# V of four batches formed from weights in SBUF, and sread's features turned once

## The chip, the cores and the metric

The kernel runs on one core of one Trainium2 chip. The metric is the device time of one execution in microseconds (us). Weights, inputs and outputs lie in the chip's DRAM; the core works on SBUF tiles of 128 partitions and collects matmul results in PSUM. Its engines are TensorE (PE, with the weight load PEld beside it), VectorE (DVE), ScalarE (ACT) and GpSimd (POOL); SyncE (SP) issues most of the DMAs of this kernel, POOL some, ACT the stores of results.

## The reference

The shapes are 8 batches, 8 heads, 512 positions, a state of 32 rows per head, D = 64, model width 512, hidden width 2048.

```python
scores = scale * np.matmul(x, state.transpose(0, 1, 3, 2))
...
xread = np.matmul(a, state)                       # a: softmax of scores
scores2 = scale * np.matmul(state, x.transpose(0, 1, 3, 2))
...
sread = np.matmul(a2, x)                          # a2: softmax of scores2
attn_out = np.concatenate([xread, sread], axis=2)
x = attn_out.transpose(0, 2, 1, 3).reshape(B * S, H * D)      # 8 x 544 tokens x 512
h = x @ w_in
g = np.where(h >= 1, h, np.where(h <= -1, 0.0, (h + 1) ** 2 / 4))
x = g @ w_out
h = x @ w2_in
g = np.maximum(h, 0.0) + alpha * np.minimum(h, 0.0)
out = g @ w2_out
```

## The kernel before, in words

The kernel has two phases. This case touches only the first: attention and the first pair of matrix products (`w_in`, `w_out`). The second phase (`hB`, `accB`) starts about half way through.

**Precision.** A float32 product is made as three matmuls on a high and a low part of each operand (high·high, high·low, low·high): `mm3`. ACT makes the high part (L73), DVE the low part (L76). Weights arrive as 64-bit floats: a raw tile `wr_…` (L302) is decoded into `wf_…` by one ACT pass (L309) and four DVE passes (L318, L320, L323, L326), then split into `w_…h` and `w_…l`.

**Stages and steps.** The first phase is 9 stages t of 16 steps f; step i = 16·t + f, and `gi(t, f)` is its number. Each step makes 128 hidden columns: `h_mm(i + 2)` fills `hA`, `act_fn` makes `g`, `g_split` its parts `gh` and `gl`, `out_mm(i)` adds to four `accA`. Stages 0 to 7 are the 512 xread rows of batches 0 to 7, stage 8 the 256 sread rows of all batches. In stage 0 the `accA` products take one matmul each (L516), from stage 1 on three (L524).

**V.** For xread the state and `w_in` are multiplied first: V[t, blk, q] = state of batch t times the 512 columns `blk` of `w_in`, four heads in each q, and `hA` is V times the attention weights `at…`. V of batch 0 is made from the parts of `w_in` in SBUF (`vdirect`). For batches 1 to 4 (group 0) and 5 to 7 (group 1) V is made in groups: `stg` holds the state of four batches, transposed and split into `sts…h` and `sts…l`. The parts of `w_in` are first stored to DRAM as `wd` (L372). For each `blk` and head, POOL loads the 64 rows of that head, high parts over low parts, into one tile `ws` (L408), PE makes two matmuls with it (L416, L417), ACT copies the result to `vgo` (L419), and SP stores that to DRAM as `vd` (L420). `vr_load` (L426) fetches the rows of one batch back when its stage is near.

**sread.** Its rows come out of the attention with the features in another order (tile `xsf`), so `w1s_load` (L450) reads 128 rows of `wd` in that order: four runs of 32 rows each per tile. 32 such loads, `w1s…h` and `w1s…l`, feed `hA` of stage 8. `xs_hi` and `xs_lo` make the parts `xsh` and `xsl`.

**What sets the order.** Side work is put at a step by `at(step, function, …)`; a loop over the steps emits it beside the main work, and a scheduler orders each engine's instructions from there. An SP DMA that has to wait for data or for a free buffer holds up all that stands behind it in SP's queue. `up` is a pool of 80 tiles of 128x512, `vp` one of 10 tiles of 128x1024 (raw weights, `x`, `x2h`, `x2l`, `stg`, `xsf`).

Of the kernel before, what the change touches and what calls it, by code (L numbers as in the profile page):

```python
# [9 lines left out]
F32 = mybir.dt.float32  # L10
# [21 lines left out]
NB, NH, S, NS, D = 8, 8, 512, 32, 64  # L32
# [8 lines left out]
def kernel_body(ctx: ExitStack, tc: tile.TileContext, x, state, w1i, w1o, w2i, w2o, alpha, out):  # L41
# [9 lines left out]
    def U(name, dt=F32):  # L51
        return up.tile([128, 512], dt, tag="u", name=name)

    def V(name, dt=F32):
        return vp.tile([128, 1024], dt, tag="v", name=name)
# [4 lines left out]
    def PS(name):  # L60
        return pp.tile([128, 512], F32, tag="ps", name=name)
# [37 lines left out]
    GRP = [1, 4]  # L99
# [6 lines left out]
    XS = {}  # L106
# [188 lines left out]
    W = {}  # L295
    VW = {}
    ST = {}
# [87 lines left out]
            VW[b, blk, q] = (h, l)  # L385

    def ld_stg(g):
        t = V(f"stg{g}")
        tv = t.rearrange("p (h u d) -> p h u d", h=NH, u=2)
        for i in range(4):  # L390
            for u in range(2):
                ld.dma_start(out=tv[32 * i:32 * i + 32, :, u, :],
                             in_=state[GRP[g] + i].rearrange("h n d -> n h d"))
        G["stg", g] = t

    def st_build(g, hh):
# [9 lines left out]
    def vg_load(g, blk, h):  # L406
        t = U(f"ws{g}{blk}{h}", F32R)
        pool.dma_start(out=t, in_=wd[blk][:, h * D:(h + 1) * D, :])  # L408
        G["w", g, blk, h] = t

    def vg_mm(g, blk, h):
        ws = G.pop(("w", g, blk, h))
        sh, sl = ST[g, h // 4]
        c = (h % 4) * 128
        ps = PS(f"vgp{g}{blk}{h}")
        pe.matmul(ps, sh[:, c:c + 128], ws, start=True, stop=False)  # L416
        pe.matmul(ps, sl[:, c:c + 128], ws, start=False, stop=True)  # L417
        o = U(f"vgo{g}{blk}{h}")
        act.copy(o, ps)  # L419
        ld.dma_start(out=vd[g][blk][h], in_=o)  # L420

    def vr_load(b, blk, q):
        g = 0 if b < 5 else 1
# [20 lines left out]

    def w1s_load(blk, c):
        h, l = U(f"w1s{blk}{c}h", F32R), U(f"w1s{blk}{c}l", F32R)
        o = (c // 2) * 256 + (c % 2) * 32
        for k, t in enumerate((h, l)):
            src = wd[blk][k, (c // 2) * 256:(c // 2 + 1) * 256, :]
            ld.dma_start(out=t.bitcast(F32), in_=src.rearrange("(h e i) f -> h e i f", h=4, e=2)[:, c % 2])  # L450
        W["w1s", blk, c] = (h, l)


# [2 lines left out]
    def gi(t, f):  # L456
        return t * NF + f
# [334 lines left out]
    def at(i, fn, *a):  # L792
        side[i].append((fn, *a))

    def xs_hi(c):
        if c == 0:
            XS["h"], XS["l"] = V("xsh", F32R), V("xsl", F32R)
        s = slice(c * 256, (c + 1) * 256)
        hi_(XS["h"][:, s], XS["f"][:, s])
# [22 lines left out]
    def vg_plan(g, start, per):  # L822
        n = 0
        for blk in range(4):
            for h in range(NH):
                o = start + int(n * per)
                at(o - 2, vg_load, g, blk, h)
                at(o + 1, vg_mm, g, blk, h)
                n += 1
        at(start - 2, ld_stg, g)  # L830
        at(start, st_build, g, 0)
        at(start, st_build, g, 1)

    vg_plan(0, gi(0, 2), 0.5)
    vg_plan(1, gi(2, 0), 1.0)

    for blk in (1, 2, 3):
# [9 lines left out]
    for f in range(NF):  # L847
        at(gi(1, f - 3), dec_hi, ("w1o", f))
        at(gi(1, f - 2), dec2, ("w1o", f))
    for c in range(4):  # L850
        at(gi(7, c), xs_hi, c)
        at(gi(7, c + 1), xs_lo, c)
    for blk in range(4):
        for c in range(4):
            at(gi(8, 4 * blk - 9 + c), w1s_load, blk, c)

    w2 = [("w2i", n // 2, n % 2) for n in range(16)] + [("w2o", f) for f in FO]
    for n, key in enumerate(w2):
        o = gi(1, 6) + int(3.2 * n)
        at(o - 3, d_load, key, src_w2p(*key[1:]) if key[0] == "w2i" else src_w2o(key[1]))  # L860
        decode(key, o)
        if key[0] == "w2i":
            at(o + 4, w2i_store, *key[1:])
        else:
            at(o + 1, w2o_put, key[1])
            at(o + 5, w2o_store, key[1])
# [91 lines left out]
```

## Time and profile before

| what | us |
|---|---|
| median of 3 runs | 1504.56 |
| lowest, highest | 1504.22, 1504.85 |
| the profiled execution | 1504.31 |
| its span | 1502.5 |
| PE busy in it | 1410.2 |
| DVE busy | 1045.4 |
| ACT busy | 782.5 |
| POOL busy | 111.2 |

The profiled execution is one run of its own; its time is the device time, its span the part between the first and the last instruction in the trace. The view by stretches cuts that span: stage 0 runs from about 34 to 190 us, stage 1 from 190 on, stage 8 from about 700 to 783. PEclk is the granted clock of TensorE as a share of its full speed. Matmuls are pipelined, so the distance between the starts of two of them, not the length of one, tells what each adds.

### The profile page before, as it was taken

The page shows a single profiled execution, that of the slowest core. Times are in us where ns is not written, and L with a number is a line of the kernel's source. Part 1 is how long each engine was busy: PE and PEld are TensorE (multiplying, and loading weights), DVE is VectorE, ACT ScalarE, POOL GpSimd, SP SyncE. Part 2 cuts the span into 40 slices and gives each one's busy share as a digit, 9 for nine tenths or more (in the row PEclk, how much of TensorE's full clock was granted, in tenths as well). Part 3 has the DMA queues.
Part 4 walks back from the last instruction along what each step waited for, and adds up shares of the span by engine and source line. Part 5 has one row for each costly group of instructions (what it writes and reads, how often), then busy time and mean ns, then how long its engine had stood idle before and what let it go on. Part 6 is the DMA issues. An engine that isn't in the chain of part 4 may idle for free.

```text
span 1502.5 us, 18956 instructions
## 1 busy us (share of the span) xinstructions
PE 1410.2 (94%) x6460; PEld 1166.7 (78%) x6460; DVE 1045.4 (70%) x1889; ACT 782.5 (52%) x1498; POOL 111.2 (7%) x125
## 2 busy tenths in 40 slices
PE   4689799899999999999779999999999999999997
PEld 2355488688888888888668878888888888989886
DVE  7687388677778788853448787666866787687641
ACT  3365577567677777764435354333533454354431
POOL 1112101112100000000110020000100010010000
PEclk8889899999999999999889999999999999999999
DMA  7999645687844444443231335344544554654554
GB/s 238 293 289 325 194 146 146 191 224 218 232 156 139 149 154 137 148 155 130 108 116 61 119 140 180 122 157 152 196 141 167 198 205 167 204 193 177 189 177 159
DMA packets 180089, 262.72 MB, mean 175 GB/s; under 512 B 76824, under 2 KB 88600, under 8 KB 179992
## 3 DMA queue, kind: packets, MB, share of 16 engines
q1 hardware_dynamic: 107720, 235.45, 46.7%
q0 software_dynamic: 66560, 17.01, 6.5%
q10 hardware_dynamic: 5712, 9.05, 1.6%
q8 instruction: 51, 0.84, 0.2%
q14 instruction: 46, 0.38, 0.1%
HBM read 205.66 MB, written 55.57 MB: 174 GB/s over the span
## 4 chain that ended last, share of the span: by engine, by line
PE 80%; DMA 10%; DVE 7%; ACT 2%; issue 1%; SPq 0%; POOL 0%; ACTq 0%; DVEq 0%; POOLq 0%
PE accB L733 22%; PE accA L524 21%; PE hB L668 20%; PE hA L84 11%; DMA wr_wi<-in_moe_w_in_dram 2%; DMA x<-in_x_dram 2%; DMA wr_w1o<-in_moe_w_out_dram 2%; PE accA L516 1%; PE sr L84 1%; PE sc L84 1%; DMA w1s33l<-wd 1%; DMA w1s13h<-wd 1%; DMA w1s23l<-wd 1%; DVE xl L76 1%; PE vgp L416 1%
## 5 line engine op out<-in xcount | busy, mean ns | idle before, releaser
L733 PE MATMUL accB<-wv,gs 128*128 128x512 f32 x1632 | 397.4, 391 | 0.2
L733 PEld LDWEIGHTS accB<-wv,gs 128*128 128x128 f32 x1632 | 305.1, 188 | 60.6 <-DVE gs L76 1.1
L668 PE MATMUL hB<-xh,wh 128*128 128x384 f32 (+1 forms) x640 | 217.9, 361 | 5.2 <-ACT p L697 2.9
L668 PE MATMUL hB<-xl,wh 128*128 128x384 f32 (+1 forms) x560 | 200.7, 358 | 0.0
L668 PE MATMUL hB<-xh,wl 128*128 128x384 f32 (+1 forms) x480 | 171.3, 360 | 0.0
L492 DVE SCALAR_TENSOR_TENSOR g<-y,hA 128x512 f32<-128x512 f32 (+1 forms) x144 | 93.6, 650 | 88.2 <-ACT y L490 87.7
L668 PEld LDWEIGHTS hB<-xh,wh 128*128 128x128 f32 x640 | 119.9, 188 | 22.5 <-DVE u L693 4.5
L76 DVE TENSOR_TENSOR gl<-g,gh 128x512 fp32r<-128x512 f32 (+1 forms) x128 | 89.1, 696 | 54.0 <-ACT gh L73 52.4
L489 ACT ACTIVATE y<-hA 128x512 f32<-128x512 f32 (+1 forms) x144 | 82.6, 574 | 73.2 <-PE hA L84 73.2
L668 PEld LDWEIGHTS hB<-xl,wh 128*128 128x128 f32 x560 | 105.5, 188 | 12.5
L677 ACT ACTIVATE m<-u 128x384 f32<-128x384 f32 (+1 forms) x80 | 45.4, 568 | 130.7 <-DVE u L693 130.7
L76 DVE TENSOR_TENSOR gs<-u,gs 128x384 fp32r<-128x384 f32 (+1 forms) x80 | 49.6, 621 | 69.5 <-ACT gs L73 69.2
L668 PEld LDWEIGHTS hB<-xh,wl 128*128 128x128 f32 x480 | 90.4, 188 | 7.8
L73 ACT CAST gh<-g 128x512 fp32r<-128x512 f32 (+1 forms) x128 | 75.7, 592 | 36.7 <-DVE g L492 31.7
L490 ACT ACTIVATE y<-y 128x512 f32<-128x512 f32 (+1 forms) x144 | 87.5, 608 | 4.2
L73 ACT CAST gs<-u 128x384 fp32r<-128x384 f32 (+1 forms) x80 | 44.4, 557 | 86.6 <-PE accB L733 85.5
L693 DVE TENSOR_TENSOR u<-hB,p 128x384 f32<-128x384 f32 (+1 forms) x80 | 48.6, 607 | 42.2 <-PE hB L668 37.4
L516 PE MATMUL accA<-g,wf_w1o 128*128 128x512 f32 x128 | 62.9, 627 | 8.1 <-DVE g L492 8.1
L679 DVE SCALAR_TENSOR_TENSOR u<-m,beta_sb,u 128x384 f32<-128x384 f32 (+1 forms) x80 | 53.4, 668 | 23.0 <-ACT m L677 22.3
L408 POOL DMA_DIRECT2D ws<-wd x64 | 50.4, 793 | 222.6 <-DMA wd<-w_wi_0l 31.0
L76 POOL TENSOR_TENSOR xl<-xr,xh 128x384 fp32r<-128x384 f32 (+1 forms) x15 | 18.7, 1247 | 630.9 <-ACT xh L73 365.2
L419 ACT COPY vgo<-vgp 128x512 f32<-128x512 f32 x64 | 36.7, 588 | 46.8 <-PE vgp L417 45.3
(916 smaller groups left out, 3045.0 us busy)
## 6 DMA issues: line engine op xcount, KB each, us to landing
wv<-wod SPq DMA_DIRECT2D x160, 512.0 KB
wr<-wid SPq DMA_DIRECT2D x80, 256.0 KB
x<-in_x_dram SPq DMA_DIRECT2D x32, 512.0 KB
ws<-wd POOLq DMA_DIRECT2D x64, 256.0 KB, 13.5
vd<-vgo SPq DMA_DIRECT2D x64, 256.0 KB
vr<-vd SPq DMA_DIRECT2D x56, 256.0 KB
out_dram<-oB SPq DMA_DIRECT2D x34, 256.0 KB
wr_wi<-in_moe_w_in_dram SPq DMA_DIRECT2D x16, 512.0 KB
```

The lines of the kernel that those rows point to most:

```text
L73: act.copy(h, raw)
L76: (eng or dve).tensor_tensor(out=l, in0=raw, in1=h.bitcast(F32), op=ALU.subtract)
L84: pe.matmul(ps, a, b, start=(k == 0), stop=(k == n - 1))
L408: pool.dma_start(out=t, in_=wd[blk][:, h * D:(h + 1) * D, :])
L489: act.activation(out=y[:, :n], in_=ps, func=AF.Relu, bias=0.5, scale=0.5)
L490: act.activation(out=y[:, :n], in_=y[:, :n], func=AF.Square)
L492: dve.scalar_tensor_tensor(out=g[:, :n], in0=y[:, :n], scalar=1.0, in1=ps, op0=ALU.min, op1=ALU.max)
L516: pe.matmul(ACC[k], w[:, k * 128:(k + 1) * 128], g, start=(f == 0), stop=(f == NF - 1))
L524: pe.matmul(ACC[k][:, :n], a, b, start=(f == 0 and j == 0), stop=(f == NF - 1 and j == 2))
L668: pe.matmul(ps, a[:, kk], b, start=(p in (0, 5, 4) and m == 0), stop=(m == 5), skip_group_check=True)
L679: dve.scalar_tensor_tensor(out=g, in0=m, scalar=beta_sb[:, f:f + 1], in1=h, op0=ALU.mult, op1=ALU.add)
L733: pe.matmul(OA[k], a, b, start=(r == 0 and j == 0), stop=(r == NF - 1 and j == 2))
```

## The change

Three things change.

First, V of group 0. `stg` is filled with zeros by POOL, and of each batch only heads of one parity are loaded into each half, so that a transposed block of `stg` has 128 rows of which 64 belong to a head and 64 are zero. With that, `vg_dir` multiplies straight with the parts of `w_in` in SBUF (128 rows, two heads), three matmuls for each head. The `ws` loads of group 0 are gone, and the matmuls for each result are three in place of two. The copy and the store stay (`vg_out`). `stg` is loaded at step −2 (was 0) and transposed at step 0 (was 2). The results come at other steps: before two heads a step from step 3 to 18, now 4, 4, 6, 6, 2, 2, 2, 2, 2, 2 heads in steps 1 to 10. Group 1 stays as it was.

Second, sread. At the last step of stage 6, `xs_turn` copies `xsf` into a new tile `xst` by 16 transfers of 32 partitions x 256 columns within SBUF, after which the features stand in their natural order; `w1s_load` reads 128 plain rows of `wd`. `xs_hi` and `xs_lo` are two steps later.

Third, the 32 decodes of the second phase's weights start at step gi(2, 4) in place of gi(1, 6), 2.75 steps apart in place of 3.2.

```diff
     def ld_stg(g):
         t = V(f"stg{g}")
         tv = t.rearrange("p (h u d) -> p h u d", h=NH, u=2)
+        if g == 0:
+            pool.memset(t, 0.0)
         for i in range(4):
             for u in range(2):
-                ld.dma_start(out=tv[32 * i:32 * i + 32, :, u, :],
-                             in_=state[GRP[g] + i].rearrange("h n d -> n h d"))
+                hs = slice(u, NH, 2) if g == 0 else slice(0, NH)
+                ld.dma_start(out=tv[32 * i:32 * i + 32, hs, u, :],
+                             in_=state[GRP[g] + i, hs].rearrange("h n d -> n h d"))
...
+    def vg_out(g, blk, h, ps):
+        o = U(f"vgo{g}{blk}{h}")
+        act.copy(o, ps)
+        ld.dma_start(out=vd[g][blk][h], in_=o)
+
+    def vg_dir(blk, c):
+        for h in (2 * c, 2 * c + 1):
+            sh, sl = ST[0, h // 4]
+            k = slice((h % 4) * 128, (h % 4) * 128 + 128)
+            ps = PS(f"vgp0{blk}{h}")
+            mm3(ps, [(sh[:, k], sl[:, k], *W["wi", blk, c])])
+            vg_out(0, blk, h, ps)
...
     def vg_mm(g, blk, h):
...
-        o = U(f"vgo{g}{blk}{h}")
-        act.copy(o, ps)
-        ld.dma_start(out=vd[g][blk][h], in_=o)
+        vg_out(g, blk, h, ps)
...
     def w1s_load(blk, c):
         h, l = U(f"w1s{blk}{c}h", F32R), U(f"w1s{blk}{c}l", F32R)
-        o = (c // 2) * 256 + (c % 2) * 32
         for k, t in enumerate((h, l)):
-            src = wd[blk][k, (c // 2) * 256:(c // 2 + 1) * 256, :]
-            ld.dma_start(out=t.bitcast(F32), in_=src.rearrange("(h e i) f -> h e i f", h=4, e=2)[:, c % 2])
+            ld.dma_start(out=t.bitcast(F32), in_=wd[blk][k, c * 128:(c + 1) * 128, :])
...
+    def xs_turn():
+        f, XS["f"] = XS["f"], V("xst")
+        for q in range(2):
+            for k in range(4):
+                for e in range(2):
+                    p, c = ((k % 2) * 2 + e) * 32, (2 * q + k // 2) * 256
+                    ld.dma_start(out=XS["f"][p:p + 32, c:c + 256],
+                                 in_=f[32 * k:32 * k + 32, (2 * q + e) * 256:(2 * q + e + 1) * 256])
...
-    vg_plan(0, gi(0, 2), 0.5)
+    at(-2, ld_stg, 0)
+    at(0, st_build, 0, 0)
+    at(0, st_build, 0, 1)
+    for blk in range(4):
+        for c in range(4):
+            at(max(1 + c, 4 * blk - 5 + c), vg_dir, blk, c)
     vg_plan(1, gi(2, 0), 1.0)
...
+    at(gi(6, 15), xs_turn)
     for c in range(4):
-        at(gi(7, c), xs_hi, c)
-        at(gi(7, c + 1), xs_lo, c)
+        at(gi(7, c + 2), xs_hi, c)
+        at(gi(7, c + 3), xs_lo, c)
...
-        o = gi(1, 6) + int(3.2 * n)
+        o = gi(2, 4) + int(2.75 * n)
```

The order of the instructions moves at three places. The rows give the line, the operation, the tile written and the tiles read; the numbers at the end of a name count the program's tiles.

First place, PE in stage 0, from the end of `hA` of step 4 on (`sc` are the attention's scores of the next batch, `stp` the transposes of `stg`, `vgp` the products of group 0). Before:

```order
L84 MATMUL hA_546<-ath_281,vw011l 128x512
L168 MATMUL sc_553<-xt_462,bdf_358 128x512
L401 MATMUL stp_562<-ident,stg_434 128x128 x4
L401 MATMUL stp_571<-ident,stg_434 128x128 x4
L516 MATMUL accA_474<-g_516,wf_w1o_403 128x512
L516 MATMUL accA_475<-g_516,wf_w1o_403 128x512
L84 MATMUL hA_611<-ath_273,vw010h 128x512
```

Now:

```order
L84 MATMUL hA_585<-ath_281,vw011l 128x512
L168 MATMUL sc_592<-xt_469,bdf_358 128x512
L168 MATMUL sc_592<-xt_477,bdf_358 128x512
L84 MATMUL vgp_597<-w_wi_1h,sts00h 128x512
L84 MATMUL vgp_597<-w_wi_1l,sts00h 128x512
L84 MATMUL vgp_597<-w_wi_1h,sts00l 128x512
L84 MATMUL vgp_604<-w_wi_1h,sts00h 128x512
L84 MATMUL vgp_604<-w_wi_1l,sts00h 128x512
L84 MATMUL vgp_604<-w_wi_1h,sts00l 128x512
L531 MATMUL accA_489<-g_473,wf_w1o_379 128x512
```

The transposes of `stg` have moved ahead of this place, and six `vgp` matmuls stand here that came later and as pairs before.

Second place, SP in stage 0, around the loads of the weights of block 2 (`wd_92` is block 1 of the stored parts). Before:

```order
L372 DMA wd_92<-w_wi_3h 128x512
L372 DMA wd_92<-w_wi_3l 128x512
L302 DMA wr_wi_2_498<-in_moe_w_in_dram 128x512
L302 DMA wr_w1o_502<-in_moe_w_out_dram 128x512
L127 DMA x_11_556<-in_x_dram 128x1024
```

Now:

```order
L372 DMA wd_92<-w_wi_3h 128x512
L420 DMA vd_0_80<-vgo_508 128x512
L420 DMA vd_0_80<-vgo_515 128x512
L420 DMA vd_1_81<-vgo_522 128x512
L420 DMA vd_1_81<-vgo_529 128x512
L372 DMA wd_92<-w_wi_3l 128x512
L302 DMA wr_wi_2_537<-in_moe_w_in_dram 128x512
L302 DMA wr_w1o_541<-in_moe_w_out_dram 128x512
L127 DMA x_11_595<-in_x_dram 128x1024
```

Four `vd` stores now stand ahead of these weight loads; before, the first `vd` store came later.

Third place, DVE in stage 1, around the pass that makes `x2l` of batch 3 (L76, 128x1024), whose end frees a buffer of `vp`. Before, in the middle of a decode of `w2i`:

```order
L318 TENSOR_SCALAR wf_w2i_1_2130<-wf_w2i_1_2130 128x512
L320 TENSOR_SCALAR wf_w2i_1_2130<-wf_w2i_1_2130 128x512
L76 TENSOR_TENSOR gl_2133<-g_2082,gh_2132 128x512
L323 SCALAR_TENSOR_TENSOR wf_w2i_1_2130<-wr_w2i_1_2040,wf_w2i_1_2130 128x512
L492 SCALAR_TENSOR_TENSOR g_2135<-y_2136,hA_2101 128x512
L76 TENSOR_TENSOR vw210l<-vr_2034,vw210h 128x512
L326 SCALAR_TENSOR_TENSOR wf_w2i_1_2130<-wr_w2i_1_2040,wf_w2i_1_2130 128x512
L76 TENSOR_TENSOR x2l_2571<-x_30_2376,x2h_2492 128x1024
```

Now:

```order
L76 TENSOR_TENSOR w_w1o_13l<-wf_w1o_1145,w_w1o_13h 128x512
L76 TENSOR_TENSOR gl_1946<-g_1891,gh_1945 128x512
L507 SCALAR_TENSOR_TENSOR g_1948<-y_1949,hA_1915 128x512
L76 TENSOR_TENSOR vw201l<-vr_1843,vw201h 128x512
L76 TENSOR_TENSOR x2l_2503<-x_30_2304,x2h_2425 128x1024
```

The pass stands behind `g` of step 32 before and behind `g` of step 29 now, and no decode of `w2i` is left ahead of it.

## Rows read from the trace of the kernel before

**Rows 1.** The page: busy time of each engine, and the granted clock in 40 equal slices of the span.

```profile
PE 1410.2 (94%) x6460; PEld 1166.7 (78%) x6460; DVE 1045.4 (70%) x1889; ACT 782.5 (52%) x1498; POOL 111.2 (7%) x125
...
PEclk8889899999999999999889999999999999999999
```

**Rows 2.** The view by stretches: start and end in us, length, busy time (and instructions) of PE, PEld, DVE, ACT and POOL, the granted clock, the DMA engines' busy share, GB/s.

```profile
34.00:78.00 44.00, 26.73 (x78) 14.69 (x76) 31.09 (x60) 17.69 (x33) 6.26 (x8) 0.87 1.19 298
78.00:108.00 30.00, 28.36 (x93) 17.33 (x94) 26.83 (x52) 19.91 (x38) 4.70 (x6) 0.90 0.92 288
108.00:160.00 52.00, 40.18 (x134) 24.59 (x133) 33.53 (x70) 25.51 (x50) 8.82 (x11) 0.93 1.09 308
160.00:190.00 30.00, 30.00 (x92) 17.59 (x91) 12.38 (x20) 18.48 (x34) 4.52 (x5) 0.96 0.63 183
190.00:290.00 100.00, 93.49 (x425) 77.23 (x425) 74.94 (x130) 70.21 (x130) 9.13 (x10) 0.97 0.50 152
507.60:572.00 64.40, 64.40 (x301) 53.76 (x300) 53.52 (x96) 45.67 (x83) 2.34 (x2) 1.00 0.44 140
700.00:783.00 83.00, 64.58 (x436) 59.81 (x435) 33.08 (x57) 31.56 (x75) 9.37 (x7) 0.88 0.30 108
```

**Rows 3.** Waits of PE in stage 8, 700 to 850 us: what waited, for what, us in total, times, the longest. The first and the last of the nine on `w1s` loads, which are 3.1, 2.3, 2.2, 2.0, 2.0, 1.8, 1.8, 1.4 and 1.1.

```profile
PE hA L84 <- DMA w1s32l<-wd: 3.1, 1, 3.1
...
PE hA L84 <- DMA w1s21l<-wd: 1.1, 1, 1.1
```

**Rows 4.** The loads of stage 8. From SP's timeline (start, length, instruction) the first issue; from the DMA view of 720 to 765 us the busy share in 40 slices (tenths) and the rates; then the mean rate of the same view of 786 to 788 us, where a load of `wr` with plain rows goes by.

```profile
667.71 0.53 SPq L450 DMA_DIRECT2D w1s00h<-wd  x1
...
DMA  2222222222222222222222232222239995222200
GB/s 102 102 102 102 102 104 100 104 102 102 102 96 104 102 102 102 102 102 102 102 102 102 102 115 104 104 102 102 95 120 279 320 224 149 98 102 102 97 35 20
...
DMA packets 265, 0.64 MB, mean 318 GB/s; under 512 B 22, under 2 KB 139, under 8 KB 265
```

**Rows 5.** PE's timeline at the start of the work on sread (start, length, instruction): two matmuls of half width in a row.

```profile
702.34 0.28 PE L84 MATMUL hA<-xsl,w1s00h 128*128 128x256 f32 x1
702.46 0.28 PE L84 MATMUL hA<-xsh,w1s00l 128*128 128x256 f32 x1
```

**Rows 6.** Stage 1: the wait of PE in 190 to 290 us, and pieces of the chain in 240 to 300 us (start, us, what).

```profile
PE accA L524 <- ACT gh L73: 6.5, 1, 6.5
...
249.87 1.37 PE hA L84 x6
...
258.97 1.24 DVE x2l L76
...
260.27 12.95 DMA x<-in_x_dram
...
275.40 4.52 PE accA L524 x12
```

**Rows 7.** Stage 0: pieces of the chain in 0 to 195 us (start, us, what).

```profile
56.83 7.40 DMA stg<-in_state_dram
...
142.88 13.21 DMA x<-in_x_dram
...
189.76 2.72 PE accA L524 x12
```

**Rows 8.** PE's timeline in stage 0: the first and the last of three groups with over 7 us of idle time before them, which stands in brackets with what ended it.

```profile
51.85 6.09 PE L516 MATMUL accA<-g,wf_w1o 128*128 128x512 f32 x8 [7.26 <-DVE g L492]
...
158.52 0.80 PE L416 MATMUL vgp<-ws,sts00h 128*128 128x512 f32 x1 [9.29 <-DVE g L492]
```

**Rows 9.** The DMA view of 0 to 160 us: all packets, POOL's queue q0 (packets, MB, time as a share of 16 engines' span), and two of the issues (count, size).

```profile
DMA packets 51351, 45.49 MB, mean 284 GB/s; under 512 B 33181, under 2 KB 36144, under 8 KB 51344
...
q0 software_dynamic: 28305, 7.18, 28.3%
...
ws<-wd POOLq DMA_DIRECT2D x28, 256.0 KB, 20.2
...
vd<-vgo SPq DMA_DIRECT2D x17, 256.0 KB
```

**Rows 10.** SP's queue in stage 0: its timeline around the loads of `stg`, and its waits for `vgo` in 0 to 190 us (us in total, times, the longest).

```profile
37.46 0.33 SPq L127 DMA_DIRECT2D x<-in_x_dram  x1
46.44 0.33 SPq L372 DMA_DIRECT2D wd<-w_wi_0h  x1
...
53.89 8.84 SPq L392 DMA_DIRECT2D stg<-in_state_dram  x8
...
SPq L420 <- ACT vgo L419: 32.2, 10, 10.1
```

**Rows 11.** The price of single instructions: one matmul of full width of group 0 from the chain at 171 us, the copy of their result (count, busy us and mean ns, idle time before it), and a zero fill on POOL.

```profile
171.72 0.23 PE vgp L416
...
L419 ACT COPY vgo<-vgp 128x512 f32<-128x512 f32 x64 | 36.7, 588 | 46.8 <-PE vgp L417 45.3
...
6.40 0.53 POOL L356 MEMSET z<- 128x512 f32 x1
```

**Rows 12.** The groups of instructions, different shapes apart: one pass of the decodes of `w2i` (count, busy us and mean ns, idle time before them).

```profile
L323 DVE SCALAR_TENSOR_TENSOR wf_w2i<-wr_w2i,wf_w2i 128x512 int32<-128x512 int32 x16 | 12.6, 790 | 0.1
```

## The prediction

> **What bounds the kernel now.** I read the page's busy line first: the matmul engine (PE) is busy 94% of the span; the granted clock is below full in two places, the first fifth and around the middle [rows 1]. Then the table by stretches: from 507 to 572 us, a piece of stage 6, PE is busy in every microsecond at full clock, and no faster transfer can shorten such a piece. There are three other places [rows 2]. Stage 0 (34 to 190 us): PE is idle for 17.3 + 1.6 + 11.8 us in the three stretches to 160 and full in the last one, at a clock of 0.87 to 0.96. Stage 1 (190 to 290): idle 6.5 us. Stage 8 (700 to 783): busy 64.6 of 83.0 us, clock 0.88. The waits of stage 8 name one cause: nine waits of PE for `w1s` tiles, from 3.1 down to 1.1 us, 17.7 us together [rows 3]. The idle time of stage 1 is one wait for `gh`, and the chain leads from there back over a single `x` load of 12.95 us, issued when a DVE pass over `x2l` freed its buffer [rows 6]. In stage 0 the chain is mostly loads, and the waits of PE in it are of 7 to 9 us each [rows 7, 8].
>
> **Stage 8: the w1s loads.** 32 loads of 256 KB. In the 45 us where hardly anything else moves, the profile has 102 GB/s at a DMA busy share of two tenths: four fifths of the engines' time lies empty [rows 4]. A load with 128 plain rows on both sides (`wr`, at 786 us) comes at 318 GB/s mean [rows 4]. So the 8.4 MB take 82 us now and would take 26 us. The first is issued at 667.7 us, the last is needed near 737 us if PE doesn't wait, so there are some 69 us: too few now, ample then. What would be late next is PE itself. Stage 8 has 384 matmuls of half width, 0.12 us apart [rows 5], and the window 52 more of full width at 0.23 us [rows 11]: 46.1 + 12.0 = 58.1 us at full clock. The whole gain is at most 83.0 − 58.1 = 24.9 us, of which 17.7 are the waits named and the rest is cold clock and small waits; a gain of the named waits alone, with the clock left as it is, would be 17.7. The clock is full in the piece of stage 6 where PE has no waits [rows 2], so I take nearly all: **−23** (−18 to −25).
>
> [...]
>
> **What is moved for it.** The features of sread are turned by 16 transfers of 32 KB at the last step of stage 6, and `xs_hi` and `xs_lo` come two steps later. 16 issues at 0.33 [rows 10] to 0.53 us [rows 4] are 5 to 9 us of SP in a stage in which no engine but PE is full; what is queued behind them are loads with several steps of lead. ACT reads the turned tile three steps later, PE 15 steps later (a step is 2.72 + 1.37 = 4.1 us [rows 6, 7]). I count them at **0**; the other end, if all 9 us held up a load that PE waits for, is +9, which I keep for the range only, since in that stage no PE wait for a load shows before.
>
> **Stage 0: V of batches 1 to 4.** Added on PE: each of the 32 products now takes three matmuls instead of two, 32 × 0.23 us = **+7.3 us** [rows 11]. Removed: 32 loads of 256 KB by POOL. What they cost is not on POOL, it is on the transfer engines. Up to 160 us, 45.49 MB go by at a mean 284 GB/s [rows 9], with a busy share of the DMA engines of 1.19, 0.92 and 1.09 in the three stretches [rows 2] (queues overlap, so it passes 1); the stretch is bound by transfers. 28 of the 32 loads lie in it, 7.3 MB. Against that, all 32 `vd` stores are now due by step 10, where 17 lay in this stretch before: +15 × 256 KB = 3.9 MB. Net 3.4 MB less, at 284 GB/s **12 us less**. The bounds: PE is idle for 30.7 us between 34 and 190 [rows 2]; the added matmuls fill 7.3 of these, and no more than the other 23.4 can be gained. On the other side, if the loads that PE waits for come no earlier, the 7.3 us of matmuls fall where PE was already full: +7.3. The order shows where they fall (first place): behind `hA` of step 4, where before stood two transposes and two `accA`, PE now has six `vgp` matmuls, and twenty heads stand in the first four steps, 60 matmuls or 13.8 us. Those are the stretches with 17.3 idle us, so most of it fills holes. The wait of 9.29 us near the end of the stage [rows 8] hangs on the `x` load of 13.21 us behind a late `wd` store [rows 7], and stays in part. I take the value that the bytes give, **−12** (−8 to −16 as its own range), net of the matmuls: it leaves 30.7 − 7.3 − 12 = 11.4 us of idle time, about that last wait and a little.
>
> The batched state `stg` now comes two steps earlier. Its eight issues held SP 8.84 us, and its landing stands in the chain with 7.40 us between two weight loads [rows 7, 10]. Before it, SP has a gap of 8.6 us between 37.8 and 46.4 [rows 10], which takes them. In the order `stg` is then ahead of the weight loads it stood between. The zero fill on POOL is twice the 0.53 us of the fill of `z` [rows 11]; POOL is idle there. On ACT the 32 copies of 588 ns [rows 11] are the same as before, only earlier. So **0** for these, with the 7.4 us of chain as an upside that is part of the bound of 23.
>
> **Stage 1.** Since the decodes of w2 start 14 steps later, DVE reaches `x2l` behind `g` of step 29 instead of 32 (order, third place). That pass releases the buffer of the late `x` load [rows 6]; three steps of 4.1 us are 12.3, the load takes 12.95, and ACT wants it at the same step as before. So the wait of 6.5 us goes all but a little, and with it the slow group behind it (12 `accA` in 4.52 us [rows 6], at full clock 2.72 [rows 7]): at most −8.3. At the least 0, if the load is held by transfers beside it. I take **−7**.
>
> **Stages 2 to 7.** The same 32 decodes are packed into 2.75 steps each instead of 3.2. DVE has 53.5 us of work in a piece of 64.4 us [rows 2]; a decode is four passes of about 0.79 us [rows 12], 3.2 us, one every 11.3 us now against 13.1 before: +2.5 us per 64 us, 87% of the time. PE stays the bound; I allow **+1** for small waits (0 to +3).
>
> **Sum.** −23 − 12 − 7 + 1 = −41 us on the profiled execution's own 1504.31 us (its span 1502.5 and 1.8 around it), which lies 0.25 us under the median of the runs: 1463.3, **about 1463 us**. With each term at its own ends: 1455 to 1474.
>
> **Rivals.**
> - Stage 0 gives nothing: SP's new order has four `vd` stores between two halves of a `wd` store and ahead of the next weight loads (order, second place), each waiting for its ACT copy (before: ten such waits, 32.2 us [rows 10]), so the loads that PE waits for come no earlier, and the added matmuls cost 0 to 7.3. For it: the stores now stand in the very steps where the weight loads are late. Against it: each load is asked for a step before its first decode and several before PE wants it, and fewer bytes go by. 1475 to 1483 us. Chance 0.17.
> - Stage 0 gives all that the PE bound allows, 22 to 23 instead of 12, since the chain's loads queue behind POOL's many small packets now (28305 of 51351 [rows 9]). Against it: the `x` load behind the last `wd` store. 1452 us. Chance 0.15.
> - The pattern of the `w1s` loads isn't what makes them slow (or the turn doesn't change it), and they stay at 102 GB/s: stage 8 gives nothing and the rest stands, 1486 us. For it only that no plain load from `wd` by SP stands in the trace before. Against it: the same queue reads plain rows at three times the rate at 786 us. Chance 0.04. [...]
> - Slower: the same SP waits as in the first rival, in full. All 32 stores at 3.2 us each are 103 us of SP time where 32 were, 71 more; it decides when over 32 us of these 71 hold up weight loads, since the other stages give 29. With half on the path, 1504 − 29 + 35 = 1510 us. Against it: most waits of SP only mirror a PE that is itself late. Chance 0.02.
>
> **How the numbers follow.** The forecast has 0.62. The range for 8 in 10: its own 1455 to 1474, down over the second rival to **1448** (that rival with stage 8 or 1 at their best) and up into the first as far as **1478**; what is left out is the upper half of the first rival and the last two. About 0.2% (3 us) is what a measurement of this kernel can tell from no change; only the last rival and a little of none reach there: faster 0.97, within 0.2% 0.01, slower 0.02.
>
> **What would show it.** Right: no PE wait for `w1s` in stage 8, its window (from the first `hA` on `w1s` to the end) at 59 to 63 us, DMA above 250 GB/s in short bursts there; `x` of stage 1 landed before ACT asks and no `gh` wait of 6 us; in stage 0 three-matmul groups in the first ten steps, no POOL loads, the first three-term `accA` of stage 1 some 12 us before 189.8 [rows 7]; DVE near 87% in stage 6 with PE still full. Wrong: `w1s` still at about 100 GB/s, or stage 0 with new SP waits on `vgo` ahead of `wr` loads and PE idle as long as now, or PE waits for `w1s` replaced by waits for `xsh`.

## The result

The changed kernel takes 1448.49 us (median of 4, 1448.31 to 1449.29), the kernel before 1504.7 beside it (1504.22 to 1505.64): a ratio of 0.9627, 95% interval 0.961 to 0.9643, so 56 us less. The forecast was 1463 with a range of 1448 to 1478; the time lies half a microsecond inside its low end.

The page of the kernel after, busy time and granted clock, as in [rows 1]:

```profile
PE 1403.4 (97%) x6492; PEld 1166.6 (81%) x6492; DVE 1050.1 (73%) x1889; ACT 782.2 (54%) x1498; POOL 87.0 (6%) x94
...
PEclk8999999999999999999999999999999999999999
```

32 matmuls more, and yet 6.8 us less of busy PE: both places of low clock in [rows 1] are gone but for the first slice.

The view by stretches of the kernel after, columns as in [rows 2]; stage 1 starts at 169.9 us here, stage 8 lies in the last row:

```profile
34.00:78.00 44.00, 35.50 (x123) 22.63 (x123) 38.77 (x75) 26.44 (x50) 1.03 (x2) 0.95 0.87 298
78.00:108.00 30.00, 29.93 (x110) 19.86 (x108) 24.69 (x49) 19.71 (x37) 0.00 (x0) 1.00 0.94 331
108.00:145.00 37.00, 37.00 (x129) 23.71 (x129) 27.47 (x53) 23.81 (x45) 1.37 (x1) 1.00 0.82 283
145.00:165.00 20.00, 20.00 (x61) 11.26 (x61) 11.48 (x20) 11.16 (x23) 1.35 (x1) 1.00 0.45 112
165.00:265.00 100.00, 100.00 (x457) 81.99 (x456) 72.34 (x121) 71.83 (x133) 8.69 (x10) 1.00 0.39 112
...
660.00:740.00 80.00, 76.72 (x517) 70.69 (x516) 45.25 (x77) 40.96 (x92) 9.46 (x7) 1.00 0.45 151
```

Compare the first four with the first four of [rows 2]: PE idles for 8.5 + 0.1 us where it idled for 30.7, the clock is full from 78 us on, and the busy share of the DMA engines now falls to 0.82 and 0.45 before the stage ends. From 165 to 265 us PE has no hole. The waits of PE in 0 to 180 us of the kernel after, the four of them in stage 0 from 34 us on (in [rows 8] single ones of 7.26 and 9.29):

```profile
PE accA L531 <- DVE g L507: 4.2, 1, 4.2
...
PE vgp L84 <- DVE g L507: 1.6, 1, 1.6
PE hA L84 <- DVE g L507: 1.4, 1, 1.4
PE hA L84 <- DVE atl L76: 1.3, 1, 1.3
```

All waits of PE in 655 to 745 us of the kernel after, and from the DMA view of 640 to 700 us the rates, which answer to [rows 3] and [rows 4]:

```profile
PE hB L683 <- ACT p L712: 2.5, 1, 2.5
PE hB L683 <- DVE m L694: 0.7, 1, 0.7
PE accA L539 <- DVE gl L76: 0.2, 1, 0.2
```

```profile
GB/s 348 191 19 11 344 274 287 388 100 0 0 0 276 363 309 300 370 391 96 83 339 270 16 0 0 0 0 180 350 326 361 280 332 258 276 96 274 75 14 161
```

No wait for `w1s` is left; the loads come in bursts of 260 to 390 GB/s, with gaps near 0 between them.

**Where the 55 us of the span went.** The first three-term `accA` of a stage marks its start in PE's timeline, and the first `accB` the second phase; the differences add up to the whole.

| stretch | before | after | difference |
|---|---|---|---|
| start to stage 1 | 189.60 | 169.93 | −19.7 |
| stage 1 | 74.50 | 72.68 | −1.8 |
| stage 2 | 87.57 | 79.23 | −8.3 |
| stage 3 | 79.14 | 79.76 | +0.6 |
| stages 4 to 6 | 215.66 | 215.66 | 0 |
| stage 7 to first `accB` | 155.04 | 129.27 | −25.8 |
| second phase | 700.99 | 700.97 | 0 |

The wait that the prediction placed in stage 1 lies by this count at the head of stage 2; it is the same wait.

### The profile page after: what moved, and what is told of

Same layout as the page of the kernel before. It is cut to its first block, busy times and chain, and to the rows that moved or that the text cites. A ratio compares the mean times of both kernels' runs of the same rounds, so it can differ in the third digit from the quotient of the medians.

```text
span 1447.5 us, 18876 instructions
## 1 busy us (share of the span) xinstructions
PE 1403.4 (97%) x6492; PEld 1166.6 (81%) x6492; DVE 1050.1 (73%) x1889; ACT 782.2 (54%) x1498; POOL 87.0 (6%) x94
## 4 chain that ended last, share of the span: by engine, by line
PE 87%; DVE 7%; DMA 2%; ACT 1%; issue 1%; POOL 0%; ACTq 0%; SPq 0%; DVEq 0%; POOLq 0%
PE accB L748 23%; PE accA L539 22%; PE hB L683 21%; PE hA L84 13%; PE accA L531 3%; PE sc L84 1%; PE sr L84 1%; PE vgp L84 1%; DVE xl L76 1%; DMA x<-in_x_dram 1%; DVE xt L649 1%; DVE gs L76 1%; DVE xt L142 0%; PE vgp L436 0%; PE vgp L435 0%
## 5 line engine op out<-in xcount | busy, mean ns | idle before, releaser
L76 DVE TENSOR_TENSOR gl<-g,gh 128x512 fp32r<-128x512 f32 (+1 forms) x128 | 92.9, 726 | 36.4 <-ACT gh L73 34.8
L76 DVE TENSOR_TENSOR gs<-u,gs 128x384 fp32r<-128x384 f32 (+1 forms) x80 | 49.6, 622 | 69.5 <-ACT gs L73 69.1
L76 POOL TENSOR_TENSOR xl<-xr,xh 128x384 fp32r<-128x384 f32 (+1 forms) x15 | 18.7, 1246 | 613.3 <-ACT xh L73 606.2
L73 ACT CAST xh<-xt 128x512 fp32r<-128x512 f32 (+1 forms) x64 | 36.4, 577 | 34.9 <-DVE xt L649 31.5
```

What stands on the lines that cost most here:

```text
L73: act.copy(h, raw)
L76: (eng or dve).tensor_tensor(out=l, in0=raw, in1=h.bitcast(F32), op=ALU.subtract)
```

## The experiments

The starts of stages in all kernels, read from PE's timeline in the same way, us:

| kernel | median | stage 1 | stage 2 | stage 3 | stage 7 | first `accB` |
|---|---|---|---|---|---|---|
| before | 1504.7 | 189.60 | 264.10 | 351.67 | 646.47 | 801.51 |
| after | 1448.49 | 169.93 | 242.61 | 321.84 | 617.26 | 746.53 |
| only_turn | 1482.81 | 190.91 | 265.43 | 354.52 | 650.51 | 779.79 |
| only_vg | 1480.34 | 169.97 | 242.66 | 329.39 | 624.19 | 777.67 |
| only_w2 | 1496.19 | 189.48 | 263.97 | 343.24 | 638.44 | 792.25 |
| runs16 | 1478.88 | 187.06 | 261.56 | 348.97 | 643.77 | 773.04 |
| w1s_quarters | 1482.47 | 191.03 | 265.53 | 353.68 | 648.76 | 780.48 |
| early_stg | 1501.49 | 188.17 | 262.67 | 350.80 | 645.60 | 799.50 |
| after_ws | 1476.21 | 196.67 | 269.36 | 348.60 | 643.47 | 772.70 |
| ws_half | 1456.97 | 177.54 | 250.25 | 329.52 | 624.56 | 753.81 |
| ws_16th | 1451.62 | 170.51 | 243.19 | 322.44 | 617.24 | 747.94 |
| after_spread | 1449.34 | 165.72 | 241.12 | 320.38 | 615.21 | 744.43 |
| mixed | 1457.86 | 175.62 | 250.22 | 329.47 | 624.28 | 754.76 |
| stg_pool | 1447.07 | 166.27 | 238.95 | 318.19 | 613.57 | 744.27 |

The start of stage 1 scatters by up to 4 us among kernels that are the same up to there (187.06 to 191.03 in the five that leave stage 0 as it was, the kernel before among them), so a difference below that in stage 0 is not read from one trace.

### One part at a time

**only_turn**: before, with sread's part alone.

```diff
-            ld.dma_start(out=t.bitcast(F32), in_=src.rearrange("(h e i) f -> h e i f", h=4, e=2)[:, c % 2])
+            ld.dma_start(out=t.bitcast(F32), in_=wd[blk][k, c * 128:(c + 1) * 128, :])
...
+    def xs_turn():
...
+    at(gi(6, 15), xs_turn)
-        at(gi(7, c), xs_hi, c)
-        at(gi(7, c + 1), xs_lo, c)
+        at(gi(7, c + 2), xs_hi, c)
+        at(gi(7, c + 3), xs_lo, c)
```

> The kernel before with sread's part alone: the features turned, w1s loaded as plain rows, xs_hi and xs_lo two steps later. If the three parts act in separate stages, everything up to the first hA on w1s (702.2 us before) stays within 1 us, the stretch from there to the end (800.3 us before) shortens by 25 to 26 us as in the changed kernel (774.5), no PE wait for w1s is left, and the time is 1478 to 1480 us. Rival, that the other parts helped stage 8 (fewer transfers ahead of it, decodes of w2 that lie elsewhere): some w1s waits stay and the time is 1482 to 1487.

1482.81 us (1480.52 to 1484.22), a ratio of 0.9856 (0.9838 to 0.9874). Stage 7 to the first `accB` takes 129.28 us, to a hundredth that of the whole change, and no `w1s` wait is left: the other parts don't help stage 8. The time is that of the rival, without its waits: the 3 us above what was expected come from elsewhere in this trace: stage 0 ends 1.3 us later, stage 2 is 1.5 longer, and stage 6, where the turn is issued, 73.1 us in place of 71.9. In the chain of that stretch the turn itself shows: a transfer of 5.39 us that ACT's `xsh` waits for, ACT work queued behind `xsh`, and then `gl`, for which PE waits 0.5 us in this stage:

```profile
620.11 5.39 DMA xst<-xsf
625.60 0.41 ACT xsh L73
...
630.97 0.67 DVE gl L76
```

In the kernel after, stage 6 has its 71.89 us. So the turn costs 0 in the whole change and up to 1.2 us in this trace, of which 0.5 is the wait; that the places of the w2 decodes make the difference was not shown.

**only_vg**: before, with `ld_stg`, `vg_dir` and the new steps of group 0 alone.

```diff
-    vg_plan(0, gi(0, 2), 0.5)
+    at(-2, ld_stg, 0)
+    at(0, st_build, 0, 0)
+    at(0, st_build, 0, 1)
+    for blk in range(4):
+        for c in range(4):
+            at(max(1 + c, 4 * blk - 5 + c), vg_dir, blk, c)
```

> The kernel before with V of batches 1 to 4 from the parts in SBUF alone (with the zero-filled stg two steps earlier). If this is what shortened stage 0, the first three-term accA comes at about 170 us (before 189.6, changed kernel 169.9), PE idles under 10 us between 34 and that point, and the time is 1482 to 1485 us (about -20 and the 2 us of work moved out of stage 1). The wait of stage 1 for its x load stays at about 6 us, since the decodes of w2 stand where they stood. Rival, that the earlier end of the transfers also frees the x load of stage 1: a further 5 to 8 us, 1475 to 1478. Rival by the prediction's term of 12 us for the bytes alone: 1490 to 1493.

1480.34 us (1479.47 to 1481.02), ratio 0.9841 (0.9826 to 0.9856). Stage 1 starts at 169.97, and the `gh` wait stays at 5.4 us, the only wait of PE in 190 to 330 us: the gain of stage 0 and the wait of stage 2 have different causes.

```profile
PE accA L541 <- ACT gh L73: 5.4, 1, 5.4
```

It is 2 us faster than expected: stage 2 is 0.8 shorter, and stage 7 to `accB` 1.6 (153.5). Eight of the nine `w1s` waits are still there, 16.9 us in place of 17.7; the cause of the rest is open.

**only_w2**: before, with the decodes moved alone.

```diff
-        o = gi(1, 6) + int(3.2 * n)
+        o = gi(2, 4) + int(2.75 * n)
```

> The kernel before with only the decodes of w2 moved (start 14 steps later, 2.75 steps apart). If they are what held the x2l pass and with it the x load, the gh wait of 6.5 us is gone, the stretch of PE from the first three-term accA of batch 2 to that of batch 3 (87.6 us before, 79.2 in the changed kernel) shortens by about 8, and the time is 1496 to 1498 us. Rival, that the x load was late because of stage 0's queue and came right through the other parts: the wait stays at 4 us or more and the time is 1501 to 1506. A second rival, that the denser decodes cost PE time in stages 3 to 7: stages of 72.5 us or more in place of 71.9.

1496.19 us (1495.03 to 1497.31), ratio 0.9946 (0.9932 to 0.9961). Stage 2 takes 79.27 us, the wait of 6.5 us is gone, and stages 4 to 6 keep their 71.9 each. The `x2l` pass and the issue of the `x` load behind it come at 244.02 and 245.30 us, where they came at 258.97 and 260.27 [rows 6] with the same start of stage 1; from DVE's and SP's timelines:

```profile
244.02 1.22 DVE L76 TENSOR_TENSOR x2l<-x,x2h 128x1024 fp32r<-128x1024 f32 x1
245.30 0.37 SPq L132 DMA_DIRECT2D x<-in_x_dram  x1
```

The first theory holds, and both rivals fall. The three parts alone give 22 + 24 + 9 = 55 us against the medians beside them, the whole change 56: they add.

### What made the w1s loads slow

**runs16**: before, the same bytes read as 16 runs of 8 rows; the sread part of the output is changed by it.

```diff
-            ld.dma_start(out=t.bitcast(F32), in_=src.rearrange("(h e i) f -> h e i f", h=4, e=2)[:, c % 2])
+            ld.dma_start(out=t.bitcast(F32), in_=src.rearrange("(h e i) f -> h e i f", h=16, e=2)[:, c % 2])
```

> The kernel before, but each w1s load takes its 128 rows of wd as 16 runs of 8 rows in place of 4 runs of 32, same bytes, not turned; the features then don't match the weights, so the sread part of the output is changed. If the rate is set by how many parts the outermost dimension of the source has (4 before), the loads speed up as with plain rows, the w1s waits go and the time is that of the turn alone, 1478 to 1481 us, without any turning. If runs of rows that don't follow each other are what costs, shorter runs are as slow or slower: 102 GB/s or less at 720 to 745 us, 1504 us or more.

1478.88 us (1475.84 to 1482.22), ratio 0.9832 (0.9812 to 0.9852). Stage 7 to `accB` 129.27 us: all of stage 8's gain, with rows more scattered than before. The rates in the DMA view of 670 to 745 us:

```profile
GB/s 11 234 227 239 270 148 1 60 238 291 288 259 262 261 257 267 68 0 0 0 319 164 386 259 281 274 264 270 30 144 138 2 9 0 0 4 0 0 0 20
```

**w1s_quarters**: before, each load cut into four of 32 plain rows.

```diff
-            ld.dma_start(out=t.bitcast(F32), in_=src.rearrange("(h e i) f -> h e i f", h=4, e=2)[:, c % 2])
+            for r in range(4):
+                ld.dma_start(out=t.bitcast(F32)[32 * r:32 * r + 32], in_=wd[blk][k, o + 64 * r:o + 64 * r + 32, :])
```

> The kernel before, each w1s load cut into four DMAs of 32 plain rows (64 KB), same rows in the same places, features not turned, result unchanged. If the number of parts of the outermost dimension sets the rate (4 in the whole load, 32 in each quarter), the w1s waits go as with the turn, first hA on w1s to first accB 73.5 to 76 us (99.3 before), 1479 to 1483 us; 128 issues at about 0.5 us are 64 us of SP in a stretch of 70, which can leave 1 to 3 us of waits. If four pieces that lie apart are slow as such, the rate stays near 102 GB/s and the time within 3 us of 1504.8.

1482.47 us (1480.6 to 1483.3), ratio 0.9855 (0.9835 to 0.9875). Stage 7 to `accB` 131.7 us: 23.3 of the 25.8 us, without a turn. Its waits of PE in 690 to 800 us that name `w1s`; its SP timeline near the end of the loads; and the rates in the DMA view of 670 to 745 us:

```profile
PE hA L84 <- DMA w1s33l<-wd: 1.3, 1, 1.3
...
PE hA L84 <- DMA w1s23l<-wd: 0.7, 1, 0.7
```

```profile
733.93 2.67 SPq L450 DMA_DIRECT2D w1s31l<-wd  x4
736.71 1.76 SPq L450 DMA_DIRECT2D w1s32h<-wd  x4
```

```profile
GB/s 218 134 151 144 138 139 145 132 142 140 140 280 210 138 142 142 56 143 238 240 145 128 0 0 161 332 243 78 138 141 145 141 139 133 85 128 152 127 150 116
```

The four issues of one load take about 1.8 us of SP, and 256 KB in 1.8 us are 146 GB/s: by these numbers it is the issuing that sets the rate here, at 140 in place of 102, and that is enough for all but 2.4 us.

So it is neither the order of the rows nor where they lie, but the shape of the transfer: an outermost dimension of 4 gave 102 GB/s [rows 4], one of 16 (runs16) or of 128 (the kernel after) gives 230 to 390 in bursts, and the quarters, with 32, went at some 140 while SP issued them. Why a pattern with 4 parts outside is slow no run here shows, and no number of parts between 4 and 16 was run.

### What made stage 0 short

**early_stg**: before, with group 0's `stg` loaded and transposed two steps earlier, nothing else.

```diff
-        at(start - 2, ld_stg, g)
-        at(start, st_build, g, 0)
-        at(start, st_build, g, 1)
+        at(start - 4 + 2 * g, ld_stg, g)
+        at(start - 2 + 2 * g, st_build, g, 0)
+        at(start - 2 + 2 * g, st_build, g, 1)
```

> The kernel before, with nothing but the load and the transposes of group 0's stg two steps earlier (step -2 and 0), full heads, ws loads kept. If stg's place between the weight loads was a cause by itself, the wait of 7.5 us of hA for vw010h at 78 us goes and the time falls by 5 to 8 us, to 1497 to 1500. If the weight load that follows it is late because of all the bytes, the wait moves elsewhere and the time stays within 2.5 us of 1504.8.

1501.49 us (1499.73 to 1504.91, 10 runs), ratio 0.9988 (0.9977 to 0.9999): by that interval 0.2 to 3.5 us, on the edge of what can be measured. The wait for `vw010h` shrank from 7.5 to 1.4 us and came back in part, most of it as 5.3 us of `hA` for `g`. The wait in the kernel before, then the four largest waits of PE in 34 to 200 us of this one:

```profile
PE hA L84 <- ACT vw010h L73: 7.5, 1, 7.5
```

```profile
PE vgp L416 <- DVE g L492: 9.2, 2, 5.6
PE accA L516 <- DVE g L492: 7.5, 1, 7.5
PE hA L84 <- DVE g L492: 5.3, 1, 5.3
PE hA L84 <- ACT vw010h L73: 1.4, 1, 1.4
```

The time lies between the two branches. The waits are those of the second, and the place of `stg` in the order is by itself worth at most some 3.5 of the 19.7 us that stage 0 gave.

**after_ws**: the kernel after, with the 32 `ws` loads issued as before into tiles that nothing reads.

```diff
+    for blk in range(4):
+        for h in range(NH):
+            at(gi(0, 2) + (blk * NH + h) // 2 - 2, vg_load, 0, blk, h)
```

> The changed kernel, with the 32 loads of ws of group 0 issued by POOL as before, into tiles that nothing reads (256 KB each, two a step). If taking these bytes and packets off the transfer engines is what shortened stage 0, most of it comes back: first three-term accA 10 to 18 us later than 169.9, PE idle over 15 us between 34 and that point, granted clock below 0.97 there, 1459 to 1468 us. If the earlier stg and products that no longer wait for a fetch did it, it stays within 4 us of 1448.5.

1476.21 us (1474.63 to 1477.06), 27.7 more than the change, and beyond the 10 to 18 expected. The start of stage 1 is 26.7 us later. The stretches of after_ws:

```profile
34.00:78.00 44.00, 31.84 (x99) 19.99 (x98) 35.94 (x69) 21.77 (x41) 8.17 (x11) 0.84 1.12 284
78.00:108.00 30.00, 27.60 (x102) 18.27 (x101) 19.16 (x39) 19.68 (x36) 6.11 (x8) 1.00 1.08 340
108.00:145.00 37.00, 33.14 (x98) 19.94 (x97) 24.63 (x49) 19.02 (x37) 7.32 (x10) 0.86 1.12 307
145.00:165.00 20.00, 16.59 (x59) 10.72 (x57) 10.18 (x18) 4.67 (x9) 2.69 (x4) 1.00 1.15 297
165.00:190.00 25.00, 21.15 (x57) 12.26 (x58) 13.74 (x23) 15.82 (x29) 4.51 (x5) 0.86 0.52 134
```

The busy share of the DMA engines is over 1 again until 165 us (1.08 to 1.15), PE idles for 25.7 us in these rows (8.6 in the kernel after up to the start of stage 1), and the clock is 0.84 to 0.86 in three of them. So some 17 of the 26.7 us are holes, and by difference the other 9.6 are matmuls that run slower.

**ws_16th** and **ws_half**: the same loads with 8 and with 64 of the 128 rows, which are one run of rows of the high parts in place of two runs, high and low (the diff is that of ws_16th; ws_half has 64 in place of 8).

```diff
-        pool.dma_start(out=t, in_=wd[blk][:, h * D:(h + 1) * D, :])
+        if g == 0:
+            pool.dma_start(out=t[:8], in_=wd[blk][0, h * D:h * D + 8, :])
+        else:
+            pool.dma_start(out=t, in_=wd[blk][:, h * D:(h + 1) * D, :])
...
+    for blk in range(4):
+        for h in range(NH):
+            at(gi(0, 2) + (blk * NH + h) // 2 - 2, vg_load, 0, blk, h)
```

> As the changed kernel with the 32 ws loads nobody reads, but each takes 8 of its 128 rows (16 KB in place of 256 KB, 0.5 MB in all): the same instructions, the same tiles taken from the pool at the same steps, the same waits of POOL for them. If the bytes and packets are what cost 27.7 us there, this one stays within 3 us of the changed kernel's 1448.5. If it is the 32 tiles that are held in SBUF, or the place of the loads in the order, most of the 27.7 stays: 1465 or more.

> The same with 64 of the 128 rows (128 KB each, 4.2 MB in all). If the price is in proportion to the bytes, at the 26.7 us that 8.4 MB cost in stage 0, it is 13 to 14 us: about 1462. If the transfers have slack to take some of them before PE runs dry, it is under 10: 1452 to 1458.

1451.62 us (1450.73 to 1454.45) and 1456.97 (1456.63 to 1458.31). With the same instructions and tiles, a sixteenth of the bytes moves the start of stage 1 by 0.6 us, half of them by 7.6, all by 26.7. So it is the transfers, not the tiles or POOL's waits (ws_16th lies 3.1 us above by the medians, just outside what was expected, of which stage 0 shows only 0.6).

By bytes the price isn't in proportion: the first 4.2 MB cost 7.6 us, the next 19.1. But the loads differ in more than bytes. POOL's queue in the DMA view of 0 to 160 us (packets, MB, time as a share of 16 engines' span) for after_ws, ws_half and ws_16th, in which 28, 28 and 29 of the 32 loads are issued by then:

```profile
q0 software_dynamic: 26647, 7.00, 27.0%
```

```profile
q0 software_dynamic: 2240, 3.67, 10.1%
```

```profile
q0 software_dynamic: 896, 0.46, 1.3%
```

The full loads go in packets of some 260 bytes on average, the half loads in packets of 1.6 KB, and 27.0% of 160 us are 43 us of all 16 engines, against 16 and 2. Per us of that time the cost is 0.62, 0.47 and 0.29 us, and the start of stage 1 scatters by up to 4 us. So it is not shown that a byte costs more when the engines are fuller, and packets and bytes were not separated.

**after_spread**: the kernel after, with its products at the old pace.

```diff
-            at(max(1 + c, 4 * blk - 5 + c), vg_dir, blk, c)
+            at(3 + 4 * blk + c, vg_dir, blk, c)
```

> The changed kernel, with the products of group 0 at two heads a step over steps 3 to 18 as before, in place of steps 1 to 10. PE work is the same. If stage 0 is now bound by PE's own work after 61 us, the place of the products matters only through holes: idle of PE before 61 us grows by up to 3 us since fewer products stand ready there, and the time is 1448 to 1452 us. If the early places are what keeps PE from waiting for weights (the 13.8 us of matmuls that fill the holes of steps 1 to 4), holes of 10 us or more open in 34 to 78 us and the time is 1455 to 1462.

1449.34 us (1447.34 to 1449.7): the same. Stage 1 starts 4.2 us earlier and is 2.7 longer, which is four heads with 12 matmuls of 0.23 us that now lie there. PE idles for under 7 us in 34 to 165. The early places of the products, and of their `vd` stores, neither help nor cost anything that can be told here. The test is a mild one for the stores: 25 of the 32 are issued by 160 us, against 32 in the kernel after, so 1.8 MB moved and not the 3.9 MB of the prediction.

### Two attempts at a better kernel

**mixed**: blocks 2 and 3 by `ws` loads and two matmuls as before, but late, from a second `stg` with full heads.

```diff
-    def ld_stg(g):
+    def ld_stg(g, z=False):
...
-        if g == 0:
+        if z:
...
-                hs = slice(u, NH, 2) if g == 0 else slice(0, NH)
+                hs = slice(u, NH, 2) if z else slice(0, NH)
...
-    at(-2, ld_stg, 0)
+    at(-2, ld_stg, 0, True)
...
-    for blk in range(4):
+    for blk in range(2):
         for c in range(4):
-            at(max(1 + c, 4 * blk - 5 + c), vg_dir, blk, c)
+            at(1 + 4 * blk + c, vg_dir, blk, c)
+    at(8, ld_stg, 0)
+    at(9, st_build, 0, 0)
+    at(9, st_build, 0, 1)
+    for n in range(16):
+        at(9 + n // 2, vg_load, 0, 2 + n // 8, n % 8)
+        at(11 + n // 2, vg_mm, 0, 2 + n // 8, n % 8)
```

> The changed kernel, with V of batches 1 to 4 for blocks 2 and 3 made as before (16 ws loads by POOL and two matmuls each, from a second stg with full heads), at steps 11 to 18, where the transfer engines have room; blocks 0 and 1 as in the changed kernel. If PE's own work sets the end of stage 0 now and transfers have slack there, it saves 16 matmuls of 0.23 us less 8 transposes: 2 to 3.5 us, 1445 to 1446.5. If the 4.7 MB added late still come into the way of the x and vr loads, it is slower than 1448.5 by 3 us or more.

1457.86 us (1457.55 to 1459.47), 9.4 more than the change: the second branch. The edit also puts the products of block 1 four steps later than in the change; after_spread moved them as well and cost nothing. Pieces of its chain in 100 to 240 us show loads one behind the other:

```profile
127.29 15.10 DMA wr_w1o<-in_moe_w_out_dram
...
147.80 7.30 DMA x<-in_x_dram
...
158.24 3.86 DMA stg<-in_state_dram
162.26 12.69 DMA ws<-wd
```

PE waits there for 6.4 us before the transposes of the second `stg`. The mean share of 0.82 from 108 to 145 us in the kernel after had looked like room; with the 16 loads of 256 KB the share there is 0.97, and PE idles for 6.6 of these 37 us, where it had no hole:

```profile
108.00:145.00 37.00, 30.42 (x101) 19.21 (x99) 20.45 (x41) 16.87 (x33) 6.15 (x7) 0.91 0.97 246
```

**stg_pool**: the kernel after, with group 0's `stg` loaded by POOL.

```diff
-                ld.dma_start(out=tv[32 * i:32 * i + 32, hs, u, :],
+                (pool if g == 0 else ld).dma_start(out=tv[32 * i:32 * i + 32, hs, u, :],
```

> The changed kernel, with the eight loads of group 0's stg issued by POOL (which zero-fills the tile just before) in place of SP, whose queue they hold for 8.65 us at 34.6 us. If that stop holds up the weight loads behind it and so the 4.2 us that PE waits for g at 48 us, part of the 8.5 us of PE idle left in 34 to 165 us goes: 1444 to 1447 us. If the weight loads behind stg wait for the decodes before them anyway, the time stays within 2 us of 1448.5.

1447.07 us (1446.11 to 1447.45, 5 runs), ratio to before 0.9618 (0.9605 to 0.9632), which overlaps that of the change (0.961 to 0.9643). Of its waits of PE in 34 to 170 us the 4.2 for `g` is still there and the later small ones are gone:

```profile
PE accA L531 <- DVE g L507: 4.2, 1, 4.2
PE hA L84 <- DVE atl L76: 0.7, 1, 0.7
```

It lies 1.4 us under the change, less than can be told here; if the gain is real, its cause isn't the expected one, since the 4.2 us stayed.

## Why the prediction came out as it did

**Stage 8** was right in mechanism and a little low in size: −23 was forecast, −25.8 came. The bound of 24.9 was all but reached; the last 1.0 us lies behind the window that it was made for, from 783 us to the first `accB`, where the clock was 0.91 before and is 1.00 now. runs16 and w1s_quarters show the cause, the shape of the source pattern: 102 GB/s with 4 parts outside, 230 and more in bursts with 16, some 140 in quarters of 32 rows. The rival that held the loads at 102 GB/s is out.

**Stage 1** (its wait for the late `x` load): −7 forecast, −8.3 measured, the upper bound. only_w2 alone gives it, with the `x2l` pass and the `x` load 15 us earlier, so that step stands.

**Stages 2 to 7**: +1 forecast, +0.6 measured, in stage 3. The turn, counted at 0, costs 0 in the whole change; only_turn has stage 6 1.2 us longer. DVE is busy 56.6 of 64.4 us in the matching piece of stage 6, 88% where 87% was forecast, and PE is full there.

**Stage 0** is the term that was mis-sized: −12 forecast, −19.7 measured, −21.5 with the 1.8 us of products moved out of stage 1. Two steps of that sum failed.

First, the bytes. "Net 3.4 MB less, at 284 GB/s" set the early `vd` stores against the `ws` loads, as if every byte had one price. [rows 9] already had another: POOL's queue took 28.3% of 160 us for 7.18 MB, which is 45 us of all 16 engines, or 158 GB/s. The hardware queue's 38.11 MB took 117 us, or 326 GB/s. That queue in the same view, before and now:

```profile
q1 hardware_dynamic: 22511, 38.11, 73.0%
```

```profile
q1 hardware_dynamic: 25835, 42.97, 80.4%
```

By this count 45 us of engine time went and 12 came (4.9 MB more on this queue), a net of 33 where the prediction counted 12. That is more than PE's idle time could give back; the transfers stopped being the bound, and PE set the end: of the 91.9 us from 78 us to stage 1 it idles for 0.1.

Second, the bound. PE's idle time was taken as all that could be gained, with its busy time fixed. The 23.4 us of that bound were not passed, but the sum behind them was incomplete. Idle time fell by 22.2 us (30.7 to 8.6, from 34 us to stage 1), the work grew by 9.1 (7.3 added, 1.8 moved in), and the end came 19.7 earlier: some 6.6 us less of busy time, since the matmuls that ran at 0.87 to 0.96 of the clock run at 0.95 up to 78 us and at full clock behind. after_ws shows the same from the other side, where 9.6 of 26.7 us are slower matmuls. The prediction used this clock in stage 8 and in stage 1 and left it out here.

The first rival (stage 0 gives nothing, at its worst +7.3) has the number that comes while the loads stay: after_ws starts stage 1 at 196.67 us, 7.1 later than the kernel before. It fell because the loads went; its own mechanism, SP's waits, is not what after_ws isolates. The second rival (stage 0 gives all that PE allows, 1452 us) is what happened, and with stages 1 and 8 also at their bounds it is 1448; its reason, POOL's many small packets, fits the engine time above, though no run separates packets from bytes. The range held by half a microsecond, and only because it was stretched over this rival; the forecast's own terms end at 1455. A margin like that is luck. The high end of those terms, 1474, was added up wrongly: with stage 1 at its own end of 0 it is 1481, and 1490 with the 9 us kept for the turn. The slow rival did not come: SP's waits for `vgo` in 0 to 180 us of the kernel after are more, but shorter than in [rows 10], 1.4 us each in place of 3.2:

```profile
SPq L420 <- ACT vgo L419: 39.1, 27, 6.2
```

## What to carry to other kernels

Where transfers fill a stretch, don't price removed bytes by the mean rate against bytes moved in: take each queue's share of the engines' time (here 158 GB/s for one queue and 326 for the other, at a mean of 284), ask whether PE becomes the bound without the removed ones, and if so take its idle time and its slow clock together (here 22.2 and 6.6 us). A load with 4 parts in the outermost dimension of its pattern ran here at 102 GB/s, where 16 or 128 parts ran at 230 to 390 in bursts; look for a low busy share beside a constant low rate (here two tenths), and try the load cut or reordered, as the change, runs16 and w1s_quarters did. And when several independent waits are removed, look how many of the bounds are reached at once: here two were, and the third to within 2 us.

## What was not expected of the hardware

Loads of 256 KB by POOL, two runs of 64 rows each, went in 1040 packets apiece (66560 for the 64 loads of the kernel before), loads of 128 KB in one run of 64 rows in 80 (2240 for the 28 of ws_half). Twice the bytes took 2.7 times the engines' time and cost 26.7 in place of 7.6 us; why the packets differ so no run here shows. And 16 of the full loads, with a second load of `stg`, cost 9.4 us, net of the matmuls that they saved, when they were added only late, from 78 us on, where the engines' share had been 0.94, 0.82 and 0.45 in the stretches up to 165 us.
